# Two steps, instead of one, in which each half of the next rows' transposes may stand, and a place behind a routing group

## The chip, the cores and the metric

The kernel runs on one core of a Trainium2 chip. The metric is the time of one execution on the device in microseconds (us), the median of several runs. The core's engines run side by side, each working through its own instructions in order: TensorE (PE; its weight loads are shown apart as PEld), VectorE (DVE), ScalarE (ACT), GpSimd (POOL) and SyncE (SP). They wait for each other at semaphores.

## What is computed

A gated recurrence along the sequence, and then a layer of eight experts on its output. The inputs are drawn with a fixed seed; B = 4, S = 5056, D = 256, so N = 20224 rows; E = 8 experts of width F = 1024.

```python
sig = 1.0 / (1.0 + np.exp(-f_logit))
f = lower_bound + (1.0 - lower_bound) * sig
for t in range(S):
    h = f[:, t] * h + (1.0 - f[:, t]) * x[:, t]
    y[:, t] = h
...
cap = N // E                      # x is y, reshaped to (N, D)
logits = x @ w_gate
# pairs (row, expert) from the highest logit down: a row goes to the first
# expert that still has room for it
...
for e in range(E):
    mask = assigned == e
    out[mask] = np.maximum(x[mask] @ w1[e], 0.0) @ w2[e]
```

## The kernel before

**Two parts.** Until about 180 us the recurrence runs, with the logits and the first expert's routing; its result is written to `hbuf` in HBM. From there to the end `moe` works through the experts, 2528 rows each. A row range of one expert is a chunk of up to four blocks of 128 rows; an expert has five chunks, expert 0 has six (of 2, 4, 4, 4, 4 and 2 blocks), the last expert six too. Each chunk takes eight steps, one for each block of 128 hidden units. I number the steps through, from 0 to 335: step 45 is the sixth step (j = 5) of the sixth chunk of expert 0, whose rows are 128 and 96.

**One step.** `first` runs six matmuls (`pw<-xh,w1h` and so on: values are split into a high and a low part, so that a product takes several matmuls) into a bank of the pool `pws`, which has three banks. ACT then writes `hh` from it (relu) and DVE `hl`; after both the bank is free again, and a new tile takes the bank that was freed first. `second` runs the second layer of an earlier step (three steps back, once under way) into `py`. The stream of these matmuls on PE is the main work.

**What is put between.** `trans` turns the next chunk's rows: four blocks are transposed by PE, one half of the 256 columns at a time (`pw<-identr,xg`, four transposes), into a bank of `pws`; ACT then writes `xh`, DVE `xl`. Each half has one fixed step, `TJ = (3, 5)`; in the first and the last chunk of the first two experts `T0 = (5, 6)`. The rows to be transposed come by `gather`: one indirect DMA on POOL for each block, `xg<-hbuf,gid`.

**Routing.** The next experts' routing runs in the background, as generators (`route`, `compact`) that `Bg.tick` advances at two points in `first`, between the blocks in `second` and at the ends of a step. A tick goes ahead only if the planner `Pace`, which adds up estimated costs of all that was written so far, finds the operands ready. A generator's piece on PE is a routing group: 20 or 23 short matmuls (`rt<-O,MK`), one to three (`rt<-RA,g`), or one (`rt<-CR,tot`). `compact` yields the row numbers `gid` (and `ids`), for three blocks at a time and for two at the start; ACT counts ranks for it (`junk<-rt,r`), DVE writes `r`, `R`, `g` and `gid`.

**POOL's queue.** Gathers, weight loads and the stores of finished rows (`out_dram<-y,ids`) wait in the list `issues`; one is issued at the end of each step and waits on the chip for the newest `hh` written so far (`paced`). So four gathers take four steps. A chunk's gathers enter the list two chunks ahead if `gid` is there; otherwise, by a fallback, in the second step of the chunk before its own.

Of the kernel before, what the change touches and what calls it, by code (L numbers as in the profile page):

```python
# [115 lines left out]
def kernel(ctx: ExitStack, tc: tile.TileContext, x: bass.AP, f_logit: bass.AP,  # L116
# [882 lines left out]
    with tc.manual_schedule(engines={mybir.EngineType.PE, mybir.EngineType.DVE, mybir.EngineType.Activation}):  # L999
        moe(ctx, tc, locals())  # L1000


def moe(ctx, tc, g):
# [28 lines left out]


    issues = []

    gate = []
    SYNC = mybir.DependencyInfo(mybir.DependencyClass.Sync, mybir.DependencyReason.DATA)

    def issue(n=1, upto=None, paced=False):
        st = None  # L1040
        if upto is not None:
            n = max([x + 1 for x, (what, _) in enumerate(issues) if upto(what)], default=0)
        for _ in range(min(n, len(issues))):
            st = issues.pop(0)[1]()
            if paced and gate:

                tc.add_manual_dep(st.ins, gate[-1].ins.name, SYNC, reason="one transfer per step")
        return st
# [29 lines left out]

    def split(k):
        issue(upto=lambda what: what == ("w", k))  # L1080
        r1, r2 = RAW[k]
        w1h = wsp.tile([P, 2, FB, P], F32R, name="w1h")
# [67 lines left out]
    posts, step = [], 0  # L1150
# [9 lines left out]
    def flush(upto=-9):  # L1160
        for p in list(posts):
            if p.at <= upto or p.ready():
                p.done = p.emit() or True
                posts.remove(p)
# [10 lines left out]
    def trans(k, c, h, now=False, between=None):  # L1175
        ns = tiles(k, c)
        w, m = sum(ns), 2 if len(ns) <= 2 else 1
        if h == 0:
            issue(upto=lambda what: what == ("g", k, c))
            XS[k, c] = (xp.tile([P, 2, 512], F32R, name="xh"), xp.tile([P, 2, 512], F32R, name="xl"))  # L1180
        elif m == 2:
            return
# [89 lines left out]
    def second(k, c, j):  # L1272
# [19 lines left out]
        for q, n in enumerate(ns):  # L1292
# [3 lines left out]
            if q:  # L1296
                tick()
# [38 lines left out]
    class Bg:  # L1336
# [3 lines left out]
        def tick(self, force=False, within=None):  # L1340
            if self.done:
                return False
            if within is not None:
                self.wait = min(self.wait, int(within))
            wants = bank in self.need
            if not force:
                if self.wait:
                    self.wait -= 1
                    return False
                if wants and bank.holder not in (None, self):  # L1350
                    return False
                tiles = [t for t in self.need[1:] if t is not bank]
                if not pace.due(self.need[0], [*tiles, *bank.last] if wants else tiles, TIGHT if closing else SLACK):
                    return False
            if wants:
                while bank.holder not in (None, self):
                    bank.holder.tick(True)
                bank.holder = self
            try:
                self.need = next(self.gen)  # L1360
                self.wait = self.apart
            except StopIteration:
                self.done = True
            return True

        def until(self, ok):
            while not ok():
                self.tick(True)

    comp, prog = {}, {}  # L1370

# [19 lines left out]
    def have(k, what, n=1):  # L1391
        return k in prog and prog[k].get(what, 0) >= n
# [47 lines left out]
    order = [(k, c) for k in range(E) for c in range(len(CHUNKS[k]))]  # L1440
# [2 lines left out]
    made = 0  # L1443
    LAG = 3
    wn = 1
    TJ, T0 = (3, 5), (5, 6)

    def rows_due(q):
        return q in comp and not comp[q].done and not have(q, "ids", NB if q == k else sum(CHUNKS[q][1]))
# [21 lines left out]
    for i in range(len(todo) + LAG):  # L1471
        step = i
        flush(i - 2 if i < len(todo) else i)
        if i < len(todo):
            k, c, j = todo[i]
            if (c, j) == (0, 0) and k:
                assert wn == k + 1
                sp.until(lambda: sp.done)
                sp = None
            first(k, c, j)  # L1480
            if i <= max(ramp):
                flush(i - 1)
                hi, lo = ramp.get(i, (None, None))
                if hi is not None:
                    high(hi)
                for n in lo or ():
                    low(n)
            tick()
            NS = len(CHUNKS[k])
            if gathers:  # L1490

                kk, cc = gathers[0]
                ahead = order.index((kk, cc)) - order.index((k, c))
                if ahead == 1 and j >= 1 or ahead == 2 and j >= (2 if (k, c) == (0, 0) else 0) and have(
                        kk, "ids", sum(CHUNKS[kk][cc])):
                    gather(kk, cc, (1, 4) if (kk, cc) == (0, 2) else None, soon=ahead == 1 or c == len(CHUNKS[k]) - 2 and j > 0)
                    gathers.pop(0)
            at = T0 if k < 2 and c in (0, NS - 1) else TJ
            nxt = order.index((k, c)) + 1
            if j in at and nxt < len(order):  # L1500
                trans(*order[nxt], at.index(j))
        while made < first_lag.get(i, i - LAG + 1):
            second(*todo[made])
            made += 1
        issue(1 if i < len(todo) else 99, paced=i < len(todo))
        tick()
# [30 lines left out]
```

## Time and profile before

| | |
|---|---|
| median of 3 runs | 1102.23 us (1101.85 to 1102.67) |
| profiled execution | 1100.87 us |
| its span | 1099.0 us |
| PE, PEld busy | 1083.8 us (99%), 959.1 us (87%) |
| DVE, ACT, POOL busy | 802.6 us (73%), 533.6 us (49%), 441.4 us (40%) |
| chain that ended last | PE 92%, DVE 2%, issue 1%, ACT 1% |

The span is the part of the execution that the trace covers. The ends of matmuls are modelled, and a matmul begins before the one ahead of it has ended; so what an instruction costs on PE is read from the starts of two that follow each other. A row of the timeline with "x4" is four equal instructions in a run.

### The profile page before, as it was taken

How to read it: one execution, taken by the hardware profiler on the slowest of the kernel's cores; microseconds unless marked ns; L12 is line 12 of the kernel's file. 1: busy time of each engine (PE TensorE's matmuls, PEld its weight loads, DVE VectorE, ACT ScalarE, POOL GpSimd, SP SyncE). 2: the span in 40 equal slices, each digit the busy share in tenths (PEclk: the TensorE clock that was granted, in tenths of full speed). 3: DMA queues.
4: the chain of work that ended last, by engine and by line, in shares of the span. 5: the costliest groups of instructions: out<-in, count | busy, mean ns of one | idle time of the engine just before them, and what ended most of it. 6: DMA issues, size and time to landing. Idle time of an engine off the chain costs nothing.

```text
span 1099.0 us, 21661 instructions
## 1 busy us (share of the span) xinstructions
PE 1083.8 (99%) x8231; PEld 959.1 (87%) x8231; DVE 802.6 (73%) x2048; ACT 533.6 (49%) x1224; POOL 441.4 (40%) x424
## 2 busy tenths in 40 slices
PE   8999999999999999999999999999999999999998
PEld 6888788999988898888888888888888888898897
DVE  7999879878877986789678867886787664334333
ACT  7999775423642544255424642364226573323323
POOL 6787403333533433343334332433334433333332
PEclk9999999999999999999999999999999999999999
DMA  9999894113111311131113111311113221111110
GB/s 372 410 398 382 318 363 146 50 43 102 59 47 44 115 48 44 43 122 47 47 44 119 49 49 43 103 65 49 43 61 107 95 74 53 48 48 51 50 42 38
DMA packets 36476, 121.74 MB, mean 111 GB/s; under 512 B 7698, under 2 KB 7700, under 8 KB 35476
## 3 DMA queue, kind: packets, MB, share of 16 engines
q0 software_dynamic: 18384, 56.12, 15.2%
q1 hardware_dynamic: 17984, 64.24, 15.0%
q8 instruction: 64, 1.05, 0.4%
q14 instruction: 40, 0.33, 0.1%
q10 hardware_dynamic: 4, 0.00, 0.0%
HBM read 78.91 MB, written 41.42 MB: 109 GB/s over the span
## 4 chain that ended last, share of the span: by engine, by line
PE 92%; DVE 2%; issue 1%; ACT 1%; DMA 0%; POOL 0%; POOLq 0%; ACTq 0%; SPq 0%
PE py L109 40%; PE pw L109 40%; PE rt L109 4%; PE pb L109 2%; PE pl L109 2%; PE pf L109 2%; PE pr L109 1%; DVE gk L109 1%; DVE MK L109 0%; DMA r<-in_moe_w_dram 0%; ACT fg L109 0%; POOL out_dram L109 0%; DVE tm L109 0%; ACT fl L109 0%; ACT y L109 0%
## 5 line engine op out<-in xcount | busy, mean ns | idle before, releaser
L109 PE MATMUL py<-w2s,hh 128*128 128x512 f32 (+3 forms) x1448 | 453.6, 366 | 1.1 <-DVE w2s L109 1.1
L109 ACT ACTIVATE hh<-pw 128x512 fp32r<-128x512 f32 (+3 forms) x336 | 192.3, 573 | 439.9 <-PE pw L109 406.8
L109 PE MATMUL py<-w2s,hl 128*128 128x256 f32 (+1 forms) x1280 | 349.4, 273 | 0.0
L109 DVE SCALAR_TENSOR_TENSOR hl<-pw,hh 128x512 fp32r<-128x512 f32 (+3 forms) x336 | 219.3, 654 | 126.0 <-ACT hh L109 124.9
L109 PEld LDWEIGHTS py<-w2s,hh 128*128 128x128 f32 (+1 forms) x1448 | 261.5, 188 | 27.3 <-DVE w2s L109 1.3
L109 POOL DMA_INDIRECT out_dram<-y,ids x160 | 161.0, 1006 | 294.8 <-ACT hh L109 148.5
L109 POOL DMA_INDIRECT xg<-hbuf,gid x160 | 163.1, 1020 | 260.7 <-ACT hh L109 204.9
L109 PE MATMUL pw<-xh,w1l 128*128 128x512 f32 (+3 forms) x672 | 248.5, 372 | 0.0
L109 PE MATMUL pw<-xl,w1h 128*128 128x512 f32 (+3 forms) x672 | 248.3, 371 | 0.0
L109 PE MATMUL pw<-xh,w1h 128*128 128x512 f32 (+3 forms) x672 | 247.2, 370 | 0.3 <-ACT xh L109 0.2
L109 PEld LDWEIGHTS py<-w2s,hl 128*128 128x128 f32 (+1 forms) x1280 | 243.4, 190 | 4.3
L109 PEld LDWEIGHTS pw<-xh,w1h 128*128 128x128 f32 x672 | 126.8, 190 | 15.9 <-ACT xh L109 0.4
L109 PEld LDWEIGHTS pw<-xh,w1l 128*128 128x128 f32 x672 | 126.9, 190 | 13.3
L109 PEld LDWEIGHTS pw<-xl,w1h 128*128 128x128 f32 x672 | 127.6, 191 | 7.0 <-DVE xl L109 0.2
L109 POOL TENSOR_TENSOR xl<-fl,xl 128x1024 f32<-128x1024 f32 (+2 forms) x39 | 91.4, 2351 | 27.9 <-ACT lg L109 5.4
L109 DVE TENSOR_TENSOR_SCAN gk<-fg,gk,pb 128x512 f32<-128x512 f32 (+3 forms) x68 | 81.6, 1241 | 9.3 <-PE pb L109 7.1
L109 ACT ACTIVATE y<-py 128x256 f32<-128x256 f32 (+2 forms) x151 | 52.7, 409 | 72.6 <-PE py L109 68.9
L109 DVE TENSOR_TENSOR y<-py,y 128x256 f32<-128x256 f32 (+1 forms) x139 | 52.9, 419 | 40.8 <-ACT y L109 38.5
L109 ACT ACTIVATE junk<-rt,r 128x158 bf16<-128x158 f32 x155 | 59.1, 395 | 20.3 <-DVE R L109 14.7
L109 ACT ACTIVATE fg<-pf,nomlb 128x512 f32<-128x512 f32 (+1 forms) x80 | 54.2, 697 | 8.1 <-DVE gk L109 3.8
L109 DVE TENSOR_TENSOR xl<-pw,xh 128x512 fp32r<-128x512 f32 (+3 forms) x81 | 54.1, 668 | 0.3 <-ACT xh L109 0.3
L109 PEld LDWEIGHTS <-MK 128*128 128x128 bf16 x1141 | 37.1, 98 | 13.9 <-issue 6.2
(224 smaller groups left out, 1268.7 us busy)
## 6 DMA issues: line engine op xcount, KB each, us to landing
fl<-in_f_logit_dram SPq DMA_DIRECT2D x39, 512.0 KB, 7.6
xl<-in_x_dram SPq DMA_DIRECT2D x39, 512.0 KB, 6.7
hbuf<-hr SPq DMA_DIRECT2D x39, 512.0 KB, 4.7
xg<-hbuf,gid POOLq DMA_INDIRECT x160, 2.8
out_dram<-y,ids POOLq DMA_INDIRECT x160, 2.4
r<-in_moe_w_dram SPq DMA_DIRECT2D x1, 1024.0 KB
r<-in_moe_w_dram SPq DMA_DIRECT2D x2, 512.0 KB, 3.8
r<-in_moe_w_dram,wi POOLq DMA_INDIRECT x21, 4.6
```

What stands on the lines that cost most here:

```text
L109: r = self.pace.last[self.name] = f(*args, **kw)
```

## The change

A half now has a range of steps. It may join from the first step of its range on, directly behind a routing group that a tick has just put on PE, if the last of its chunk's gathers was issued at least three steps ago (`landed`); if no group comes, it stands at the end of the range, where `turn_next` puts it without that condition. The two halves keep at least one step between them. `TJ` becomes (3 to 4) and (5 to 6); `T0` stays at 5 and 6.

```diff
@@ issue
-            st = issues.pop(0)[1]()
+            what, emit = issues.pop(0)
+            st = emit()
+            if what[0] == "g":
+                issued[what[1:]] = step
@@ Bg.tick
+            small = self.need[0] == "PE"
             try:
                 self.need = next(self.gen)
                 self.wait = self.apart
             except StopIteration:
                 self.done = True
+            if small:
+                join()
             return True
...
+    turns = []
+
+    def landed(kc):
+        return issued.get(kc, step) <= step - 3 and not any(what == ("g", *kc) for what, _ in issues)
+
+    def join():
+        if turns and turns[0][0] <= step and landed(tuple(turns[0][2:4])):
+            turn_next()
+
+    def turn_next():
+        trans(*turns[0][2:])
+        turns.pop(0)
+        if turns:
+            turns[0][0] = max(turns[0][0], step + 1)
...
-    TJ, T0 = (3, 5), (5, 6)
+    TJ, T0 = ((3, 4), (5, 6)), ((5, 5), (6, 6))
...
-            at = T0 if k < 2 and c in (0, NS - 1) else TJ
             nxt = order.index((k, c)) + 1
-            if j in at and nxt < len(order):
-                trans(*order[nxt], at.index(j))
+            if j == 0 and nxt < len(order):
+                span = T0 if k < 2 and c in (0, NS - 1) else TJ
+                turns.extend([i + a, i + b, *order[nxt], h] for h, (a, b) in enumerate(span))
+            if turns and turns[0][1] <= i:
+                turn_next()
```

On PE, in step 6, a join looks like this (`g` and `RA` are the routing group, `xh`, `xl` with `w1` the six matmuls of `first`, cut to a few here):

```order
 L109 LDWEIGHTS g_3246
 L109 MATMUL rt<-RA,g_3246 128x160
+L109 MATMUL pw<-identr,xg 128x128 x4
 L109 MATMUL pw<-xh,w1l 128x256 x2
 L109 MATMUL pw<-xl,w1h 128x256 x2
-L109 MATMUL pw<-identr,xg 128x128 x4
 L109 MATMUL py<-w2s,hh 128x256 x2
 L109 MATMUL py<-w2s,hl 128x256
```

The four transposes moved from behind the step's own matmuls to a place among them, right behind the group. Over the whole program PE leaves its stream of matmuls 241 times before and 206 times now: of the 79 halves with four transposes 8 stood directly behind a group by chance, now 43 do. The number of instructions of each kind stays the same.

Because the planner's sums run differently after each such move, it also places the routing in other steps. On DVE, before, around the end of expert 0's fifth chunk; `hl` is written once a step, here those of steps 38, 39 and 40, and the first `gid` holds the row numbers of expert 1's blocks 2 and 3:

```order
L109 SCALAR_TENSOR_TENSOR hl_4690<-pw_4671,hh_4689 128x512
L109 SCALAR_TENSOR_TENSOR gid_2380<-r_4680,R2_4585 128x2
L109 TENSOR_TENSOR TMP_2387<-X_162,M0_164 128x640
L109 TENSOR_TENSOR r_4720<-sq_149,rt_4716 128x3
L109 TENSOR_SCALAR R2_4585<-rt_4716 128x3
L109 TENSOR_SCALAR g1_4723<-IO_107,st_4584 128x384
L109 TENSOR_TENSOR TMP_2387<-TMP_2387,kc_119 128x640
L109 SCALAR_TENSOR_TENSOR w1l_4538<-r1_4532,omlb_113,w1h_4537 128x512
L109 SCALAR_TENSOR_TENSOR hl_4728<-pw_4710,hh_4727 128x512
L109 SCALAR_TENSOR_TENSOR hl_4762<-pw_4748,hh_4761 128x224
```

Now, with the `hl` of steps 39, 40 and 41:

```order
L109 SCALAR_TENSOR_TENSOR hl_4705<-pw_4692,hh_4704 128x512
L109 TENSOR_TENSOR r_4721<-sq_149,rt_4718 128x2
L109 TENSOR_SCALAR R2_4623<-rt_4718 128x2
L109 TENSOR_SCALAR g1_4724<-IO_107,st_4622 128x384
L109 SCALAR_TENSOR_TENSOR w1l_4579<-r1_4573,omlb_113,w1h_4578 128x512
L109 SCALAR_TENSOR_TENSOR hl_4739<-pw_4731,hh_4738 128x224
L109 TENSOR_TENSOR TMP_2387<-TMP_2387,kc_119 128x640
L109 SCALAR_TENSOR_TENSOR w1l_4579<-r1_4573,omlb_113,w1h_4578 128x512
L109 SCALAR_TENSOR_TENSOR hl_4769<-pw_4759,hh_4768 128x224
L109 SCALAR_TENSOR_TENSOR gid_2380<-r_4721,R2_4623 128x2
```

The row numbers of these two blocks moved from behind step 38 to behind step 41.

On ACT, before, from the `hh` of step 42 to the `xh` of the half that PE transposes in step 45; the `hh` of step 42 (hh_4829) is what the fourth gather for that half waits for:

```order
L109 ACTIVATE hh_4829<-pw_4816 128x224
L109 ACTIVATE y_4835<-py_4574 128x512
L109 ACTIVATE y_4843<-py_4594 128x512
L109 ACTIVATE hh_4859<-pw_4852 128x224
L109 ACTIVATE w2s_4539<-r2_4533 128x4x128
L109 ACTIVATE hh_4888<-pw_4881 128x224
L109 ACTIVATE w2s_4539<-r2_4533 128x4x128
L109 ACTIVATE hh_4910<-pw_4900 128x224
L109 ACTIVATE xh_4914<-pw_4916 128x512
```

Now, from the `hh` of step 43 (hh_4833) on; the fourth gather waits for that of step 44 (hh_4862):

```order
L109 ACTIVATE hh_4833<-pw_4821 128x224
L109 ACTIVATE junk_4840,r_4824<-rt_4780,r_4824 128x158
L109 ACTIVATE junk_4842,r_4824<-rt_4780,r_4824 128x158
L109 ACTIVATE junk_4844,r_4824<-rt_4780,r_4824 128x158
L109 ACTIVATE w2s_4580<-r2_4574 128x4x128
L109 ACTIVATE hh_4862<-pw_4855 128x224
L109 ACTIVATE w2s_4580<-r2_4574 128x4x128
L109 ACTIVATE hh_4882<-pw_4873 128x224
L109 ACTIVATE xh_4886<-pw_4888 128x512
```

The instruction that releases the fourth gather moved from three steps ahead of the transposes to one step ahead of them, and three rank counts stand in front of it.

## Rows read from the trace of the kernel before

**Rows 1.** Stretches: busy us (instructions) of PE, PEld, DVE, ACT, POOL; PEclk; DMA.
```profile
180.00:184.00 4.00, 2.92 (x26) 2.62 (x24) 3.71 (x7) 2.51 (x7) 2.07 (x2) 1.00 0.49 153
200.00:330.00 130.00, 130.00 (x1081) 119.88 (x1081) 104.74 (x300) 53.75 (x123) 49.50 (x48) 1.00 0.18 60
330.00:1090.00 760.00, 759.96 (x4993) 674.38 (x4992) 524.78 (x1398) 318.23 (x762) 281.35 (x286) 1.00 0.19 63
```

**Rows 2.** Timeline of PE (start, us, operation): a half's transposes alone.
```profile
607.17 0.38 PE L109 MATMUL pw<-xh,w1l 128*128 128x512 f32 x1
607.38 0.44 PE L109 MATMUL pw<-identr,xg 128*128 128x128 f32 x4
607.66 0.47 PE L109 MATMUL py<-w2s,hh 128*128 128x512 f32 x1
607.96 0.27 PE L109 MATMUL py<-w2s,hl 128*128 128x256 f32 x1
```

**Rows 3.** Timeline of PE: a routing group with the transposes behind it.
```profile
312.03 0.38 PE L109 MATMUL pw<-xh,w1l 128*128 128x512 f32 x1
312.25 0.76 PE L109 MATMUL rt<-O,MK 128*128 128x64 bf16 x20
312.84 0.51 PE L109 MATMUL pw<-identr,xg 128*128 128x128 f32 x4
...
313.48 0.27 PE L109 MATMUL py<-w2s,hl 128*128 128x256 f32 x1
```

**Rows 4.** Timeline of PE: around a routing group of 20 alone.
```profile
317.93 0.38 PE L109 MATMUL pw<-xh,w1h 128*128 128x512 f32 x1
...
319.05 0.38 PE L109 MATMUL pw<-xh,w1l 128*128 128x512 f32 x1
```

**Rows 5.** Timeline of POOL: transfers, with what released them.
```profile
291.71 0.98 POOL L109 DMA_INDIRECT out_dram<-y,ids  x1 [0.57 <-ACT hh L109]
...
307.64 0.96 POOL L109 DMA_INDIRECT xg<-hbuf,gid  x1 [1.58 <-ACT hh L109]
```

**Rows 6.** The 15 gathers from 270 to 330 us: issue to landing.
```profile
DMA to landing us min/median/max: 2.7/2.8/3.7
```

**Rows 7.** Timeline of PE: steps 43 to 45, and 52 and 53.
```profile
289.66 0.38 PE L109 MATMUL rt<-RA,g 128*128 128x160 bf16 x3
...
290.22 0.26 PE L109 MATMUL pw<-xh,w1h 128*128 128x224 f32 x1
...
292.21 0.47 PE L109 MATMUL pw<-identr,xg 128*128 128x128 f32 x4
...
305.01 0.38 PE L109 MATMUL pw<-xh,w1h 128*128 128x512 f32 x1
...
309.22 0.52 PE L109 MATMUL pw<-identr,xg 128*128 128x128 f32 x4
```

**Rows 8.** Timeline of ACT: steps 41 to 44.
```profile
285.74 0.80 ACT L109 ACTIVATE w2s<-r 128x512 fp32r<-128x512 f32 x1
286.42 0.40 ACT L109 ACTIVATE junk<-rt,r 128x158 bf16<-128x158 f32 x1
...
287.52 0.38 ACT L109 ACTIVATE hh<-pw 128x224 fp32r<-128x224 f32 x1
...
289.51 0.36 ACT L109 ACTIVATE hh<-pw 128x224 fp32r<-128x224 f32 x1
...
291.08 0.36 ACT L109 ACTIVATE hh<-pw 128x224 fp32r<-128x224 f32 x1 [0.58 <-PE pw L109]
```

**Rows 9.** Timeline of DVE: an `hl`, and a group's `r` up to the next work.
```profile
291.47 0.39 DVE L109 SCALAR_TENSOR_TENSOR hl<-pw,hh 128x224 fp32r<-128x224 f32 x1 [1.18 <-ACT hh L109]
...
297.12 0.15 DVE L109 TENSOR_TENSOR r<-sq,rt 128x3 f32<-128x3 f32 x1
...
297.58 0.82 DVE L109 TENSOR_TENSOR TMP<-X,M 128x640 f32<-128x640 f32 x1
```

**Rows 10.** Waits of PE's weight loads, 175 to 200 us: total, times, longest.
```profile
PEld pw L109 <- DVE hl L109: 0.2, 1, 0.2
```

More of the change, by code (lines that the diff above doesn't have):

```diff
@@ L1034, in moe @@
     issues = []
+    issued = {}
     gate = []
```

## The prediction

> **What bounds the kernel now.** I read the table of stretches first, to see whether any engine but PE has a say. From 200 to 330 us PE is busy all of the 130.00 us, from 330 to 1090 us 759.96 of 760, at a granted clock of 1.00, the 2.4 GHz level; VectorE has 105 and 525 us of work there, ScalarE less [rows 1]. So in the part that the change touches, PE never waits, and the end is set by two things alone: how much PE time the instructions take in their order, and whether a new order makes PE wait for the first time. The first I price from the timeline of PE, the second by following in the order what the moved instructions wait for, and then reading in the timelines of POOL, ACT and DVE how long that takes.
>
> **What a join saves.** A matmul of 512 columns starts 0.215 us after the one ahead (607.17 to 607.38) [rows 2]. A half alone: from the last matmul ahead (607.17) to the second one behind (607.96) are 0.79 us; without the half they would be two times 0.215, so it costs 0.36 us [rows 2]. A group of 20 alone: 317.93 to 319.05 is 1.12 us, less 0.43, so 0.69 [rows 4]. The group with the half behind it: 312.03 to 313.48 is 1.45 us, less 0.43, so 1.02 [rows 3]. Apart they cost 1.05, joined 1.02: a join saves 0.03 us. It saves so little because the four transposes and the twenty short matmuls cost their own time either way, and only one return to the stream falls away. Rows are rounded to 0.01, so I allow 0.01 to 0.05. The order has 43 joins instead of 8: 35 x 0.03 = **1.05 us less** (0.35 to 1.75). Nothing else becomes cheaper on PE: the instructions are the same in number and kind.
>
> **What the moved half costs beside PE.** Its `xh` (ACT) and `xl` (DVE) are the same work, up to one step later. The tightest regular case has the second half in step 6 of eight; ahead of its first use PE still has one `first` and two `second` to do, about as much as the 4.2 us from 305.01 to 309.22 hold [rows 7], for two instructions of at most 0.8 us (the `w2s` of the same size [rows 8]). So I cost it at nothing. It would cost something only where ACT or DVE is behind.
>
> **What is moved along with it: the gathers of expert 1.** Here the order shows a change that the diff does not: routing for expert 1 is placed some two steps later, the row numbers of blocks 2 and 3 come behind step 41 instead of 38, and so the gathers of its first chunk enter POOL's list only by the fallback, in step 41. They are issued one a step, in steps 41, 42, 43 and 44; before it was 39 to 42. The transposes stay in step 45, since `T0` has its end there and the end does not ask `landed`. Each gather waits for the `hh` of its own step. Before, the fourth waited for the `hh` of step 42, which ends at 287.90; a transfer begins 0.27 us behind its `hh` (291.71, behind 291.08 and 0.36 [rows 5, 8]), so at 288.17, and lands 2.8 us later [rows 6], at 290.97. The transposes start at 292.21 [rows 7], 1.2 us after that. Now it stands where the store of 291.71 stood, released by the `hh` of step 44 [rows 5], and lands at 294.5, while PE needs it for the last of the four transposes, about 0.2 us behind 292.21. That is a wait of 2.1 us. There is more: ACT has three rank counts and a `w2s` between the `hh` of steps 43 and 44 now. The three take 1.10 us (286.42 to 287.52), the `w2s` 0.68 (285.74 to 286.42), the `hh` itself 0.36; from 289.51 that gives 291.65 for the `hh` of step 44 instead of 291.08 [rows 8], 0.57 later. **Wait A, in step 45: 2.7 us**. Low end 2.0 (no delay on ACT, landing after 2.7), high end 3.5 (the longest landing, 3.7 [rows 6]). Behind the waiting transpose stands PE's whole stream, so this is on the path in full.
>
> On the price of a gather the Trainium skill says something else: its page "DMA: Bandwidth & Descriptors", section "Anatomy of one DMA — SWDGE (gpsimd) path", fits about 2.0 us plus the bytes at 436 GB/s, an estimate of 2.3 us for the 128 KB here. The trace has 2.7 to 3.7 [rows 6], so I keep 2.8; by the page's figure the waits A and C below would each be 0.5 us shorter and the result 1105.2.
>
> **Wait B, in step 47.** The first half's `xl` and the `hl` of step 46 now stand on DVE behind the `r`, `R` and `g` of a group that PE runs in step 46, and step 47 takes the bank that this `hl` frees. From the group's start to the next step are 0.56 us (289.66 to 290.22), the group ends after 0.38 [rows 7]; then `r` to the end of `g` take 0.46 (297.12 to 297.58) and the `hl` 0.39 [rows 9]: 1.23 less 0.56, **0.7 us** (0.3 if DVE is a little ahead, 1.0 if it is behind).
>
> **Wait C, in step 53.** The next chunk's gathers are issued in steps 49 to 52 (before: 47 to 50), and its first half stands in step 53 as before. The transfer released by the `hh` of step 52 began at 307.64 [rows 5]; landed 2.8 us later it is 310.44, the last transpose would start at 309.42 [rows 7]: **1.0 us** (0.9 to 1.9). From step 59 on the order has at least three steps between the last gather and the transposes, mostly five or six, so there is nothing more of this kind.
>
> **Small waits for a bank.** In ten chunks the two halves now stand in steps 4 and 5, one apart, and the second takes the bank that the `hl` of step 4 must free; before they were two apart. The trace has one wait of weight loads for an `hl`, of 0.2 us, in the crowded start [rows 10]. Ten times that bounds it at 2.0; below nothing it cannot go, since PE has no waits left to lose there. I take three, **0.6 us**, because DVE is a fifth idle in that stretch [rows 1].
>
> **The sum.** -1.05 + 2.7 + 0.7 + 1.0 + 0.6 = **+3.95 us**. Against the profiled execution (1100.87 us, of which 1.87 lie outside the span) that makes 1104.8; this execution lies 1.36 us below the median of the runs, and the changed kernel's median should lie as much above its own, so 1102.23 + 3.95 = **1106.2 us**. All ends together give +1.45 to +8.05; that all fall on one side is unlikely.
>
> **The rivals.** *No new wait.* If `gid` or the `hh` come earlier on the chip than the order suggests, or the four transposes are held by something else anyway, only the joins are left: 1102.23 - 1.05 = 1101.2. For it speaks that PE waits nowhere now; against it, that from the start of step 44 to the transposes of step 45 PE has 2.0 us of work (290.22 to 292.21 [rows 7]), while `hh`, issue and landing take 4.3 (to 291.71, and 2.8 [rows 5, 6]). *Joins worth more.* This is the case on the other side: a join may save the whole return to the stream. Behind the half, the first matmul of the stream keeps its follower waiting for 0.30 us (607.66 to 607.96) instead of 0.215 [rows 2]: 0.085 us of the 0.36 belong to the return. If each of the 35 joins saved that, 3.0 us would go, and if no wait came with it, 1099.2. On its own it decides from 0.063 us a join on (2.2 / 35). Against it stands the joined case itself, at 1.02 [rows 3]. *The clock.* After wait A the granted clock could fall to the 1.2 GHz level, and the stream take twice as long for a while; if that lasts for as much work as the wait was long, it costs 2.7 us more, 1108.9. Against it: from 180 to 184 us PE was busy for 2.92 of 4.00 us, and the granted clock stayed at 1.00 [rows 1]. The Trainium skill, "TensorE: Matmul & The Clock Gate", section "HAM oscillation — how this bites in real kernels", tells of a kernel whose clock fell in just such waits for transfers. *The change doesn't do what it says*: in the last experts there is no routing, and no half joins there; that is in the count of 35 already.
>
> **How the numbers follow.** The forecast, late gathers costing more than the joins give, has a chance of 0.79; no new wait 0.12; the clock 0.05; joins worth more 0.04. A measurement of this kernel can tell about 0.2%, 2.2 us, from no change. The forecast's part below +2.2 us (A alone, say, with the rest hidden) is 0.07; so slower 0.72 + 0.05 = 0.77, same 0.07 + 0.12 = 0.19, faster 0.04. The range from 1103.0 to 1109.5 leaves out the two rivals on the lower side and the outermost 0.04 of the forecast, 0.20 together.
>
> **What would show it.** In the profile after: among PE's waits a new one of 2 to 3.5 us for `xg<-hbuf,gid` near 290 us, and a second of about 1 us some 17 us later; a wait for `hl` between them; PE no longer busy all of the stretch from 200 to 330, but 759 of 760 us in a stretch as long behind it. A group of 20 with a half behind it again 1.02. The prediction is wrong if PE shows no wait for `xg` there, if the joined pieces come out at 0.95 or less, or if the waits for banks add up to more than 2 us.

## The result, and the profile after

| | before | after |
|---|---|---|
| median | 1102.54 us (6 runs, 1101.85 to 1103.83) | 1108.18 us (6 runs, 1105.79 to 1111.54) |
| ratio | | 1.0052, 95% interval 1.0039 to 1.0065 |
| profiled execution, span | 1100.87, 1099.0 us | 1111.54, 1109.0 us |

The change makes the kernel 5.6 us slower. The forecast was 1106.2, 2.0 us less than the 1108.18. Of these, 0.3 are the median of the kernel before, which six executions put at 1102.54 and not at 1102.23; so 1.7 us are to be explained beside the 3.95 that the forecast had.

PE's waits over the whole span of the changed kernel (total us, times, longest), those that the kernel before has not or hardly has:

```profile
PE pw L109 <- DMA xg<-hbuf,gid: 3.5, 4, 1.8
PE pw L109 <- ACT xh L109: 2.3, 1, 2.3
...
PE pw L109 <- DVE hl L109: 1.0, 3, 0.3
```

The kernel before waits 0.2 us for `xg` and for `xh` and never for `hl`. The stretches of rows 1, after (busy us of PE, PEld, DVE, ACT and POOL, then the granted clock and the DMA share):

```profile
180.00:184.00 4.00, 3.75 (x19) 3.75 (x20) 2.30 (x4) 2.24 (x5) 1.91 (x2) 0.57 0.88 319
200.00:330.00 130.00, 126.47 (x1022) 116.18 (x1021) 100.23 (x285) 54.81 (x130) 42.38 (x44) 0.99 0.17 57
330.00:1090.00 760.00, 759.31 (x5005) 674.78 (x5004) 528.75 (x1416) 319.84 (x760) 286.34 (x290) 1.00 0.19 63
```

From 200 to 330 us PE is idle for 3.5 us, where it was never idle before. Behind 330 us it is idle for 0.7 of 760 us. And there is something that the sum of the forecast left out: the first row has a granted clock of 0.57, and the second a mean of 0.99 instead of 1.00.

The place of wait A on PE's timeline (start, us, operation, and in brackets the idle time ahead and what ended it), step 45's transposes, step 46, and the start of step 47:

```profile
295.69 0.29 PE L109 MATMUL pw<-identr,xg 128*128 128x128 f32 x2
296.62 0.28 PE L109 MATMUL pw<-identr,xg 128*128 128x128 f32 x1 [0.63 <-DMA xg<-hbuf,gid]
298.71 0.28 PE L109 MATMUL pw<-identr,xg 128*128 128x128 f32 x1 [1.81 <-DMA xg<-hbuf,gid]
...
299.55 0.26 PE L109 MATMUL pw<-xh,w1h 128*128 128x224 f32 x1
299.65 0.36 PE L109 MATMUL pw<-xl,w1h 128*128 128x224 f32 x1
299.81 0.42 PE L109 MATMUL pw<-xh,w1l 128*128 128x224 f32 x1
300.02 0.42 PE L109 MATMUL pw<-xh,w1h 128*128 128x224 f32 x1
...
303.48 0.36 PE L109 MATMUL pw<-xh,w1h 128*128 128x224 f32 x1 [0.28 <-DVE hl L109]
```

The two transposes of the first two blocks run, the third waits 0.63 us for its gather, the fourth 1.81. Then something that no wait explains: from one matmul of 224 columns to the next are 0.10 us at first (299.55 to 299.65), but 0.21 from 299.81 to 300.02. The granted clock, in stretches of 2 us, says why:

```profile
298.00:300.00 2.00, 1.29 (x10) 1.30 (x11) 0.00 (x0) 0.60 (x1) 0.14 (x1) 0.93 0.20 78
300.00:302.00 2.00, 2.00 (x13) 1.91 (x12) 0.00 (x0) 0.95 (x2) 0.45 (x1) 0.50 0.00 0
302.00:304.00 2.00, 1.72 (x11) 1.37 (x11) 1.43 (x6) 0.00 (x0) 0.55 (x1) 0.72 0.16 66
```

About 1 us after the wait (298.71) the clock falls to its lower level, 1.2 GHz, and stays there for some 3.4 us: 0.3, 2.0 and 1.1 us of the three stretches, by their means of 0.93, 0.50 and 0.72.

What held the fourth gather, on ACT and on POOL, and how long the gathers from 285 to 325 us took to land; these rows answer to rows 5, 6 and 8:

```profile
293.23 0.36 ACT L109 ACTIVATE hh<-pw 128x224 fp32r<-128x224 f32 x1
...
295.25 0.37 ACT L109 ACTIVATE hh<-pw 128x224 fp32r<-128x224 f32 x1
```

```profile
295.89 0.94 POOL L109 DMA_INDIRECT xg<-hbuf,gid  x1 [1.09 <-ACT hh L109]
```

```profile
DMA to landing us min/median/max: 2.6/2.7/3.0
```

The first ACT row is the `hh` of step 43, the second that of step 44; the three rank counts and the `w2s` stand between them. The `hh` of step 44 ends at 295.62, the transfer begins 0.27 us later, and the transpose that needs it starts 2.82 us after that, at 298.71. Wait C, in step 53, and one of two waits for a bank further on:

```profile
318.30 0.43 PE L109 MATMUL pw<-identr,xg 128*128 128x128 f32 x3
319.52 0.28 PE L109 MATMUL pw<-identr,xg 128*128 128x128 f32 x1 [0.78 <-DMA xg<-hbuf,gid]
...
716.21 0.53 PE L109 MATMUL pw<-identr,xg 128*128 128x128 f32 x4 [0.34 <-DVE hl L109]
```

And a join, as in rows 3:

```profile
343.00 0.38 PE L109 MATMUL pw<-xh,w1h 128*128 128x512 f32 x1
343.22 0.76 PE L109 MATMUL rt<-O,MK 128*128 128x64 bf16 x20
343.81 0.51 PE L109 MATMUL pw<-identr,xg 128*128 128x128 f32 x4
...
344.44 0.38 PE L109 MATMUL pw<-xh,w1l 128*128 128x512 f32 x1
```

From 343.00 to the second matmul behind, 344.44, are 1.44 us, less two times 0.215: 1.01. All 14 of this kind give 1.017 in the median; the 35 halves that still stand alone give 0.364, and the groups of 20 alone 0.679. So a join is worth 0.364 + 0.679 - 1.017 = 0.026 us. By the same sum the joins behind two or three short matmuls give about as much, and the 11 behind a single one 0.015; the 35 new ones are worth 0.8 to 0.9 us together.

**Where the 10 us between the two profiled executions are.** For each step I take the start of its first matmul in the trace, less the start of the same step in the trace of before. The columns are steps; 335 is the last.

| trace | 0 | 4 | 45 | 46 | 47 | 53 | 54 | 335 |
|---|---|---|---|---|---|---|---|---|
| after | 2.71 | 3.97 | 3.48 | 6.31 | 8.55 | 9.08 | 10.07 | 10.02 |
| half_release | 0.23 | 0.27 | -0.23 | 0.56 | 1.57 | 2.10 | 2.10 | 2.03 |
| late_look | 0.74 | 0.88 | 0.90 | 2.98 | 4.35 | 4.55 | 5.61 | 5.58 |
| early_release | 3.92 | 5.51 | 5.05 | 5.06 | 6.07 | 6.61 | 6.61 | 8.62 |
| filled_wait | 3.89 | 5.48 | 4.99 | 7.76 | 8.77 | 9.31 | 10.23 | 12.15 |
| after_again | 4.00 | 5.70 | 5.10 | 8.63 | 10.58 | 11.12 | 12.04 | 14.02 |
| before_again | 4.07 | 5.76 | 6.28 | 6.28 | 6.28 | 6.28 | 6.28 | 8.10 |

The other lines are the experiments below. In the changed kernel's line: 3.97 us are lost by step 4, in code that is the same in both kernels; 2.83 from step 45 to 46 (wait A), 2.24 to step 47, 0.53 from there to step 53, 0.99 from 53 to 54 (wait C), and nothing in sum behind that. The 0.53 (or 0.54) stand in all five traces of the changed order (after, half_release, early_release, filled_wait, after_again); 0.44 of them are in step 48, where a routing group of three now stands, and 0.10 in step 47. Three questions follow: does the late start belong to the change; is it the gathers, and they alone, that cost the rest; and what are the joins worth.

The runs were made on several chips, on some of which every kernel starts its step 0 late; each ratio below is against the kernel before on the same chip, and is an estimate of its own, not the quotient of the two medians. One of the nine executions of late_gathers, 1574.89 us at a granted clock of 0.65, is left out of its median.

### The profile page after: what moved, and what is told of

It reads as the page before. It is cut to its first block, busy times and chain, and to the rows that moved or that the text cites. A ratio compares the mean times of both kernels' runs of the same rounds, so it can differ in the third digit from the quotient of the medians.

```text
span 1109.0 us, 21644 instructions
## 1 busy us (share of the span) xinstructions
PE 1088.0 (98%) x8231; PEld 964.4 (87%) x8231; DVE 801.7 (72%) x2048; ACT 536.1 (48%) x1224; POOL 439.4 (40%) x424
## 3 DMA queue, kind: packets, MB, share of 16 engines
q8 instruction: 64, 1.05, 0.4%
## 4 chain that ended last, share of the span: by engine, by line
PE 87%; DVE 4%; DMA 3%; issue 3%; ACT 1%; POOL 1%; SPq 0%; POOLq 0%; ACTq 0%
PE pw L109 38%; PE py L109 37%; PE rt L109 4%; PE pb L109 2%; PE pl L109 2%; PE pf L109 2%; PE pr L109 1%; DMA fl<-in_f_logit_dram 1%; DVE hl L109 1%; DMA xl<-in_x_dram 1%; DMA r<-in_moe_w_dram 1%; DVE gk L109 1%; DMA xg<-hbuf,gid 0%; DMA out_dram<-y,ids 0%; POOL xg L109 0%
## 5 line engine op out<-in xcount | busy, mean ns | idle before, releaser
L109 ACT ACTIVATE xh<-pw 128x512 fp32r<-128x512 f32 (+3 forms) x81 | 47.4, 586 | 52.1 <-PE pw L109 51.6
```

Of the source, the lines that this page charges most:

```text
L109: r = self.pace.last[self.name] = f(*args, **kw)
```

## The experiments

### The same kernels once more: after_again, before_again

> The changed kernel once more, for the comparison with the three kernels that run beside it, and to see which of its stretches come again. Theory: wait A (step 45, four waits of 2.4 us in sum for the gathers), wait C (step 53, 0.8 us) and two small waits for a bank (0.3 us each near 716 and 832 us) stand in every execution, since the orders set them; the stretch at half clock behind wait A (2.1 us longer in steps 46 and 47) and the late start of step 0 (2.7 us, and 1.0 us at half clock behind it) come in some executions only. So executions at a granted clock of 1.000 take 1105 to 1106.5 us, those at 0.998 or less 1107 to 1111. Rival: the late start belongs to the change, then it stands in this profile again, with 2 to 3 us of waiting for xh near 178 us.

Measured: 1115.54 us against 1108.94 for the kernel before, ratio 1.0066 (1.0053 to 1.0080). Waits A (0.64 and 1.77 us), the half clock behind it and C stand again, at the same steps. The expected times are missed, as this chip adds 6.4 us to the kernel before as well (1108.94 against 1102.54). All six executions had a granted clock under 1.000, so this chip gave no undisturbed one.

> The kernel before, once more, for its steps on the chip on which the three kernels beside it run. Theory: on a chip where step 0 starts late, the kernel before starts late too, since the code up to there is the same in all of them: 2 to 4 us of waiting for xh or the first rows near 178 us and some us at half clock behind it, and nothing of this kind near 290 us. Rival: it starts at 177.5 us again, and the late start belongs to the change.

Measured: 1109.12 us, and step 0 starts 4.07 us later than in the first trace of the same kernel. Stretches of before_again around step 0:

```profile
178.00:180.00 2.00, 0.00 (x0) 0.00 (x0) 0.42 (x1) 1.03 (x2) 1.55 (x2) 1.00 0.99 361
...
182.00:184.00 2.00, 2.00 (x11) 2.00 (x11) 1.36 (x3) 0.91 (x3) 0.00 (x0) 0.50 0.23 70
...
186.00:188.00 2.00, 1.96 (x11) 1.67 (x10) 1.72 (x3) 1.66 (x4) 0.00 (x0) 0.60 0.00 0
```

PE waits with the DMA engines full, and from its step 0 (181.6) to about 187.6 it runs at half clock, some 6 us. The kernel before does this too. So the late start is no part of the change: it comes with the chip and the execution, costs 4 to 7.5 us by step 4 where it comes, and the profiled execution of the changed kernel had a mild one.

### The gathers earlier again: early_release, half_release

```diff
-                tc.add_manual_dep(st.ins, gate[-1].ins.name, SYNC, reason="one transfer per step")
+                tc.add_manual_dep(st.ins, gate[-3 if 41 <= step <= 44 or 49 <= step <= 52 else -1].ins.name, SYNC,
+                                  reason="one transfer per step")
```

`gate` holds the `hh` instructions; half_release has -2 in place of -3. PE, DVE and ACT keep the changed kernel's order.

> The changed kernel with one thing taken back: the gathers issued in steps 41 to 44 and 49 to 52 wait for the hh of two steps before, as they did ahead of the change (the row numbers still come when they come). PE, DVE and ACT have the same order. Theory (the loss is waits A and C, and the clock that falls behind A): no wait of PE for xg over 0.3 us near 296 and 319 us, granted clock 1.00 from 290 to 310 us, and 3.3 us less than the changed kernel's undisturbed executions, 5 to 6 less than those with the clock fall: 1101.5 to 1103.5, within 0.2% of the kernel before. Rival (the moved routing and transposes cost by themselves, or a new wait takes the place): 1105 to 1108, as the changed kernel.

Measured: 1109.56 us, ratio 1.0014 (1.0004 to 1.0023), 6.0 us less than after_again on the same chip. In the table step 46 comes 0.01 us late against step 45, and nothing is lost from 53 to 54: A, C and the half clock are gone. On the first chip the ratio would make 1104.1, 0.6 above what was expected, since the expectation had no wait B in it; so its rival, that the moved routing costs by itself, holds in a small part. From 46 to 47 the kernel still loses 1.01 us (PE and DVE; "issue" is a wait for which the profile names nothing):

```profile
300.12 0.27 PE L109 MATMUL py<-w2s,hl 128*96 128x256 f32 x1
301.00 0.36 PE L109 MATMUL pw<-xh,w1h 128*128 128x224 f32 x1 [0.61 <-issue]
```

```profile
300.09 0.16 DVE L109 TENSOR_TENSOR r<-sq,rt 128x3 f32<-128x3 f32 x1 [1.45 <-PE rt L109]
...
300.24 0.41 DVE L109 TENSOR_SCALAR g<-IO,st 128x384 bf16<-128x384 f32 x1
300.56 0.38 DVE L109 SCALAR_TENSOR_TENSOR hl<-pw,hh 128x224 fp32r<-128x224 f32 x1
```

The first row of PE's and the last of DVE's belong together: the last matmul ahead of step 47 starts at 300.12 and would be followed 0.11 us later; step 47 starts at 301.00, when the `hl` of step 46 (to 300.94) has freed the bank. That is wait B, 0.77 us, and it stands on DVE behind `r`, `R` and `g` as the forecast had it. The other 0.24 of the 1.01 are a routing group that stood in step 43 before; from step 43 to 44 the trace has the same 0.24 with the other sign.

> The changed kernel with the gathers of steps 41 to 44 and 49 to 52 waiting for the hh of one step before instead of the newest: half of what early_release takes back, with the same order on every engine. Theory (wait A is the distance from the release of the fourth gather to the transposes, and the half clock follows from the length of PE's idle time there): a step at that place is 2.0 us, so A shrinks from 2.7 to 0.7 us, C from 0.9 to 0, and an idle time of 0.7 us leaves the clock at 1.00 (as wait C of 0.8 us did): step 47 begins about 4 us sooner than in after_again against the same step 40, and B (0.8 us) stays. Rival (the clock falls with any wait there, or A is set by the landing and not by the release): half clock again, 2 us or less taken back.

Measured: 1103.08 us against 1101.42, ratio 1.0013 (1.0001 to 1.0025), on a chip without the late start.

```profile
292.95 0.28 PE L109 MATMUL pw<-identr,xg 128*128 128x128 f32 x1 [0.59 <-DMA xg<-hbuf,gid]
...
296.50 0.36 PE L109 MATMUL pw<-xh,w1h 128*128 128x224 f32 x1 [0.60 <-DVE hl L109]
```

```profile
294.00:298.00 4.00, 3.40 (x32) 3.15 (x31) 2.20 (x7) 1.44 (x5) 1.03 (x2) 1.00 0.16 66
```

Released one step (2.0 us) earlier, wait A shrinks from 2.83 to 0.79 us in the table, the clock stays at 1.00, C is gone and B stays at 0.77. From step 40 on this trace is the cleanest account of the change without its late gathers: 2.03 us at the end, of which 0.23 were there at step 0.

### The late gathers alone: late_gathers, late_look

```diff
-                if ahead == 1 and j >= 1 or ahead == 2 and j >= (2 if (k, c) == (0, 0) else 0) and have(
+                if ahead == 1 and j >= 1 or ahead == 2 and (kk, cc) not in ((1, 0), (1, 1)) and j >= (
+                        2 if (k, c) == (0, 0) else 0) and have(
```

This is put into the kernel before.

> The kernel before with one thing put in: the gathers of expert 1's first two chunks are issued in steps 41 to 44 and 49 to 52 instead of 39 to 42 and 47 to 50; PE, DVE and ACT keep the order of before, no transpose joins a group. Theory: waits A (2.4 to 2.8 us) and C (0.8 to 1.0 us) appear, with the clock at half for 2 to 4 us behind A in some executions: 1106 us without the clock fall, up to 1108.5 with it. Rival (the waits are hidden by something that only the joins or the moved routing take away): under 1104.

Measured: 1111.99 us against 1108.94, ratio 1.0038 (1.0020 to 1.0057), which is 4.2 us. The same kernel once more, for its profile:

> The kernel of late_gathers once more, for a profile of it at full clock. Theory: from step 40 to step 46 2.5 to 3 us more than the kernel before (wait A), waits of PE for xg near 296 us and, 0.8 to 1.0 us, at step 53; behind A 2 to 4 us at half clock, about 2 us more by step 48; wait B does not appear, since DVE keeps the order of before. Rival: the transposes wait less than 1 us in sum.

Measured: 1106.61 us in one run, against 1101.42.

```profile
293.81 0.28 PE L109 MATMUL pw<-identr,xg 128*128 128x128 f32 x1 [0.41 <-DMA xg<-hbuf,gid]
295.37 0.28 PE L109 MATMUL pw<-identr,xg 128*128 128x128 f32 x1 [1.28 <-DMA xg<-hbuf,gid]
```

```profile
296.00:298.00 2.00, 2.00 (x15) 2.00 (x13) 0.69 (x1) 0.64 (x2) 0.00 (x0) 0.57 0.00 0
298.00:300.00 2.00, 2.00 (x12) 2.00 (x12) 1.96 (x4) 0.61 (x2) 0.99 (x1) 0.57 0.07 31
```

Two of the forecast's steps come apart here. Wait A is 2.08 us in the table, under the 2.5 to 3 expected, and not 2.83: in this kernel ACT has no three rank counts ahead of the `hh` of step 44, which the forecast priced at 0.57 of its 2.7, and the routing group stays in step 43. And there is no wait B, as DVE keeps its order: the 1.57 us from step 46 to 53 are half clock alone. C is 1.06. So the late gathers by themselves, without any join, make 4.7 us from step 45 to 54.

### The clock: filled_wait

```diff
         for q, n in enumerate(ns):
+            if (k, c, h) == (1, 0, 0) and q > 1:
+                for _ in range((0, 0, 6, 18)[q]):
+                    tc.nc.tensor.matmul(pt[:, 0, q * P:].bitcast(F32), g["bz"][:, :P], g["bz"][:, :512 - q * P],
+                                        start=True, stop=True)
             for i in range(m):
```

> The changed kernel with 24 matmuls of zeros put between the transposes of step 45: 6 of 256 columns ahead of the third block, 18 of 128 columns ahead of the fourth, into columns of the bank that the transposes write afterwards. The wait for the gathers stays, but PE works through most of it. Theory (the half clock behind wait A comes from PE's idle time in it): granted clock 1.00 from 296 to 306 us in the profile, steps 46 and 47 without the 100 ns more on each matmul of 224 or 256 columns, wait A's end where it was; 1105 to 1106.5 us, with no executions above that but for a late start. Rival (the clock falls with something else, or the work put in delays the transposes): half clock there again, or 1 to 2 us more at step 45.

Measured: 1113.17 us, ratio 1.0050 (1.0036 to 1.0065), 2.4 us less than after_again on the same chip.

```profile
298.00:300.00 2.00, 1.38 (x21) 1.13 (x19) 0.52 (x3) 0.00 (x0) 1.34 (x2) 1.00 0.21 66
300.00:302.00 2.00, 1.84 (x18) 1.84 (x18) 0.00 (x0) 0.73 (x2) 0.00 (x0) 1.00 0.16 66
```

Wait A is as long as ever (2.77 us from step 45 to 46), but the clock stays at 1.00, and from 46 to 47 only the 1.01 us of wait B and the moved group are left. Against after_again (3.53 and 1.95) that is 0.76 and 0.94: the half clock cost 1.7 us there. In the profile after, where step 47 came 2.24 us later, it cost 2.24 - 1.01 = 1.2: the clock is at half as long there, but part of wait B passes meanwhile, so that only 0.28 us of it are seen (303.48). In late_look it cost 1.6. One profile could have missed the fall by chance, as the fall does not come in every execution (below); but all five executions of filled_wait have a granted clock of 0.996 or 0.997, and four of the six of after_again 0.994 or 0.995. The expected time was for a chip without the late start; the rest came as expected.

### The price of leaving the stream: singles

In the kernel before, `trans` writes one transpose at once and the others one by one behind the next matmuls of `first` and `second`:

```diff
-        for q, n in enumerate(ns):
-            for i in range(m):
...
+        apart.extend((one_of, (q, n, i)) for q, n in enumerate(ns) for i in range(m))
+        apart.append((posts_of, ()))
+        one_at_a_time()
```

> The kernel before with the four transposes of every half put one by one, each behind another matmul of the stream: PE leaves the stream 318 minus 84 = 234 times more, with the same instructions. It doubles the disputed price 234 times, where the change takes it away 35 times. Theory (leaving and coming back costs 0.026 us: 0.364 for four alone against 0.338 behind a group): 234 x 0.026 = 6.1 us more than before, one transpose alone 0.11 us. By the ends of the forecast's bounds: 0.01 gives 2.3 us, 0.05 gives 11.7 us. Rival (a join saves nothing, the difference is the way the ends are modelled): within 1 us of before, one transpose alone 0.085 us. What the banks' later release adds is read from the waits for hl.

```profile
642.09 0.37 PE L109 MATMUL pw<-xh,w1l 128*128 128x480 f32 x1
642.29 0.23 PE L109 MATMUL pw<-identr,xg 128*128 128x128 f32 x1
642.35 0.43 PE L109 MATMUL py<-w2s,hh 128*128 128x512 f32 x1
642.62 0.23 PE L109 MATMUL pw<-identr,xg 128*128 128x128 f32 x1
...
643.38 0.38 PE L109 MATMUL py<-w2s,hh 128*128 128x512 f32 x1
```

Four transposes with a matmul between each: from 642.09 to the fifth matmul, 643.38, are 1.29 us; the five matmuls that start in it would take 0.86, so the half costs 0.43. Over all 65 halves of this kind the median is 0.442, against 0.364 in one piece: three more times out of the stream cost 0.078 us, **0.026 each**. The time is 1117.67 us against 1108.78, ratio 1.0072 (1.0049 to 1.0095), 8.0 us (8.9 by the medians): 234 x 0.026 = 6.1, and behind 190 us the trace has 2.0 us of waits for `xg` and one of 0.8 for which the profile names nothing, neither of which is in before_again. The price is what it was taken for; the rival of nothing and the end of 0.05 are both out.

### Joins without the late gathers: later_joins, later_apart_2, held_85, held_57

```diff
-        if turns and turns[0][0] <= step and landed(tuple(turns[0][2:4])):
+        if step >= 48 and turns and turns[0][0] <= step and landed(tuple(turns[0][2:4])):
...
-                span = T0 if k < 2 and c in (0, NS - 1) else TJ
+                span = T0 if k < 2 and c in (0, NS - 1) else TJ if k else ((3, 3), (5, 5))
```

> The changed kernel with joins and ranges from step 48 on alone; in the steps of expert 0 the halves stand at 3 and 5 as before. The planner then runs as before up to there, the gathers of expert 1's first two chunks are issued in steps 39 to 42 and 47 to 50, and 27 halves fewer stand alone instead of 35 fewer. Theory (all of the loss hangs on the moved row numbers of expert 1, the joins are worth 0.026 us each): no waits A, B and C, no half clock near 300 us; 27 x 0.026 = 0.7 us gained, two small waits for a bank of 0.3 us each may stay: 0.1 to 0.7 us under the kernel before on the same chip. Rival (joins cost something by themselves further on, by the bank that the transposes hold or by ACT and DVE): 1 us or more over it.

Measured: 1108.81 us against 1108.78, ratio 1.0002 (0.9989 to 1.0015). Nothing is lost near 300 us: its steps 45, 46, 47, 53 and 54 are all late by 8.11 or 8.12 us, of which 7.53 were there at step 4 (before_again loses as much on the way, 5.76 to 6.28). Behind 330 us the profile has its two waits for a bank:

```profile
PE pw L109 <- DVE hl L109: 0.6, 2, 0.3
```

So without A, B and C the change is worth nothing that can be measured; 0.7 us of joins stand against 0.6 of waits for a bank. The next kernel has `step + 2` in place of `step + 1` in `turn_next`:

> The kernel of later_joins with the two halves of a chunk at least two steps apart (25 halves fewer stand alone). Theory (the small waits for a bank come from halves in steps 4 and 5): no wait of PE for hl of 0.3 us behind step 48, 0.65 us gained on the kernel before and up to 0.6 us on later_joins. Rival (the small waits come from other work on DVE at that place): the same waits again, and the time of later_joins.

Measured: 1113.41 us against 1108.78, ratio 1.0043 (1.0027 to 1.0058). The waits for `hl` are gone, as expected, but there is another:

```profile
PE py L109 <- DVE y L109: 2.4, 2, 1.2
```

```profile
659.09 0.78 DVE L109 TENSOR_TENSOR MK<-K,TH 128x1200 bf16<-128x1200 int16 x1
...
660.39 0.74 DVE L109 TENSOR_TENSOR y<-py,y 128x256 f32<-128x256 f32 x2
```

At two ends of chunks DVE now has a piece of routing (`MK`, 0.78 us, and short ones ahead of it) in front of the `y` that frees a bank of `py`, and PE waits 1.2 us for it each time. That the small waits are gone fits their cause, though the routing moved too. Taking them away cost 4.6 us; these two waits show 2.4 of them, and the rest is not traced.

In the last two, made from the kernel before, a half is called up at its old step and held until the next routing group, one step at the most; the planner counts it where it was called:

```diff
-                trans(*order[nxt], at.index(j))
+                held.append((i, (*order[nxt], at.index(j))))
+                pace.free["PE"] += HELD
```

> The kernel before with another way to join: each half is called up at its step of before (3 and 5, or 5 and 6), the planner's sum counts it there (85 ns for each transpose), and it is written directly behind the next routing group, at the latest one step on. The row numbers come no later than before, every chunk's gathers are issued three steps or more ahead of its first transposes, 38 halves fewer stand alone (242 places where PE leaves the stream become 204), and the two halves of a chunk stand in neighbouring steps in 8 chunks instead of 14. Theory (the joins are worth 0.026 us each and only what the planner moves behind them costs): no waits A, B and C, 38 x 0.026 = 1.0 us less than before, of which waits for a bank take 0 to 0.6: ratio 0.999 to 1.000. Rival (holding back a half costs as much as it saves, by ACT and DVE that write xh and xl later): 1 to 4 us more than before, with waits for y, hl or xh in the profile, as in later_apart_2.

> The kernel of held_85 with 57 ns for each transpose in the planner's sum, the value of its own cost table: 40 halves fewer stand alone, the row numbers come one to three steps later than in held_85, no chunk's gathers less than three steps ahead. Theory: 40 x 0.026 = 1.0 us less than before, no waits A, B and C, waits for a bank 0 to 0.6 us. Rival: as for held_85; and if the two differ by more than 1 us, it is the planner's placing of the routing that decides and not the joins.

Measured: 1120.72 us (held_85) and 1117.63 (held_57) against 1113.46; ratios 1.0063 (1.0047 to 1.0079) and 1.0045 (1.0028 to 1.0063). Waits of PE in held_85:

```profile
PE pw L109 <- DVE xl L109: 3.3, 4, 2.3
PE py L109 <- DVE y L109: 2.8, 3, 1.2
```

The theory is wrong here and the rival right: PE waits four times for an `xl`, once for 2.3 us, and `y` is late again. 38 and 40 joins are in, worth 1.0 us, and the kernel is 5 to 7 us slower. Apart from each other the two lie 3.1 us, with a number in the planner's sum as the only edit; a part of that is the clock. Both profiles have the wait of 2.3 us, in one piece, ahead of a half's transposes. In held_85 the clock falls behind it, about 1.2 us after work is resumed:

```profile
197.10 0.54 PE L109 MATMUL pw<-identr,xg 128*128 128x128 f32 x4 [2.32 <-DVE xl L109]
```

```profile
198.00:200.00 2.00, 2.00 (x11) 1.82 (x10) 1.70 (x6) 1.01 (x5) 0.95 (x1) 0.57 0.00 0
```

In held_57 it does not, in this stretch or the next:

```profile
195.69 0.53 PE L109 MATMUL pw<-identr,xg 128*128 128x128 f32 x4 [2.29 <-DVE xl L109]
```

```profile
196.00:198.00 2.00, 2.00 (x17) 1.92 (x17) 1.11 (x5) 0.90 (x2) 0.57 (x1) 1.00 0.00 0
```

So the length of a wait does not settle by itself whether the clock falls behind it; what else decides stays open.

No version here beats the kernel before. With all of the 71 halves that stand alone in it joined and nothing else moved, 1.8 us would be the most to gain, less than a measurement tells from nothing.

## Why the prediction was right, and where it was 2 us short

| term | forecast | measured | where |
|---|---|---|---|
| joins | -1.05 | -0.8 to -0.9 (35 x 0.026 at most) | groups of the trace after, singles |
| wait A | 2.7 | 2.83 | step 45 to 46, after |
| wait B | 0.7 | 0.77 | early_release, half_release |
| wait C | 1.0 | 0.99 | step 53 to 54, after |
| small waits for a bank | 0.6 | 0.7 | 0.34 and 0.35 us, after |
| half clock behind A | 0, as a rival 2.7 | 1.2 to 1.7 | after, late_look, filled_wait against after_again |

**The mechanism and the five terms of the sum hold.** Wait A had two parts in the forecast: 2.1 us by the later release, which late_look shows alone (2.08), and 0.57 by the three rank counts on ACT. Of the latter 0.45 came: from the `hh` of step 43 to that of step 44 are 2.02 us after (293.23 to 295.25) and 1.57 before [rows 8]. Another 0.24 that the forecast did not have come from the routing group that left step 43: PE is at the transposes that much sooner and waits that much longer, and what is won ahead is lost there. The 0.27 us from `hh` to transfer and the 2.8 to landing came as read from rows 5 and 6. By the Trainium skill's page "DMA: Bandwidth & Descriptors", section "Anatomy of one DMA — SWDGE (gpsimd) path", a landing takes 2.3 us, an estimate from its fit, 0.5 less than the 2.8; the trace (2.6 to 3.0) does not agree. That the third gather would be late too (0.63) was not said; it takes nothing from the sum, since the fourth comes behind it. Of the small waits there are fewer than allowed for, and they are longer: two of 0.35 us instead of three of 0.2. In sum the terms give 4.4 us, with 1.2 for the clock 5.6; from step 4 to the end the trace after loses 10.02 - 3.97 = 6.05, so some 0.4 us are in no term, and the 0.53 in steps 47 to 52, a cost of the moved routing, are the likely place. half_release says the same: 1.80 us from step 0 to the end, where its terms (A 0.79, B, the small waits, the joins) give 1.35.

**What failed is the step that argued the clock away.** The rival was there with its mechanism, but the chance of 0.05 rested on one row: from 180 to 184 us PE was idle for 1.08 of 4 us and the clock stayed at 1.00 [rows 1]. That was one wait of 1.1 us, and is no evidence for an idle time of 2.4. The runs show both sides: behind idle times of 0.6 and 0.8 us (half_release, wait C) the clock stayed at 1.00; behind 0.41 and 1.28 with a transpose between (late_look), behind 0.63 and 1.81 (after), and around the waits of 2.3 us and more at a late start it fell to 0.5. In between it goes both ways: behind one wait of 2.3 us it fell in held_85 and held in held_57, and one of the six executions of the changed kernel, which all have wait A in their order, shows a granted clock of 1.000. So a chance well above 0.05 was due, and not certainty. That PE's idleness is the cause is what filled_wait tests: with work put into the wait, the clock held. The Trainium skill, "TensorE: Matmul & The Clock Gate", section "HAM oscillation — how this bites in real kernels", describes a wait for a transfer that sends the next piece of work off at half clock. The traces agree that it happens, behind shorter waits than those of that page's kernel. The price of the half clock was too high in the forecast, 2.7 us against 1.2 to 1.7.

**Where luck had a part.** The measured 1108.18 us lies nearer to this rival's 1108.9 than to the forecast's 1106.2. It fell into the stated range because the range, drawn for the ends of the waits, reached over the rival too.

**The spread of the executions** goes with the clock: 1105.79 us for the one at a granted clock of 1.000, which by that has no half clock, and so probably no late start, and lies 0.4 us from the forecast, up to 1111.54 for the profiled one, at 0.997, which has both. The late start was in no row of before, and before_again shows that it could have been.

**The other rivals.** "No new wait" fell with the first row of waits. "Joins worth more" fell with 1.017 and with singles: the return to the stream is paid once behind a joined piece too, and what a join saves is 0.026 of the 0.085 us by which the matmul behind a half is late. That the joins don't happen fell with the 14 joined groups of 20.

## What to carry over

A rule that moves work to a cheaper place moves everything that a planner sets by it; follow what the moved instructions release and wait for before pricing the saving, here 0.9 us saved against about 5 lost on gathers whose consumer had a fixed place. If a consumer's place is fixed, test the distance to its producer there too: `landed` guarded the beginning of each range and not its end. And when an engine waits for the first time, price the wait and what the clock does behind it; evidence that the clock held through a shorter wait doesn't cover a longer one, and one profile in which it held or fell doesn't settle the next.

## What the runs showed of the chip

- Wait A in PE's stream (2.4 us idle in after and after_again, 1.7 in late_look, each in two pieces) cost more than itself: the clock fell to its half level about 1 us after work was resumed (after, late_look) or just as it was (after_again) and stayed there for 3.4 us, which cost 1.2 to 1.7 us. 24 matmuls of zeros in the wait kept it up. A single wait of 2.3 us went either way (held_85, held_57).
- The kernel before starts its expert part at 177.5 us in one trace and at 181.6 in another (before_again), there with PE idle, the DMA engines at 0.99 of their time, and half clock behind it. Its medians were 1101.4 and 1102.5 us in two sets of runs and 1108.8 to 1113.5 in three others, of which two, 1108.8 and 1113.5, were on one chip. A single profile shows one of these cases.
- Leaving a stream of wide matmuls for transposes and coming back costs 0.026 us each time here: four transposes take 0.364 us together and 0.442 one by one.
